# The last columns of wq's last slot, loaded as eight loads of eight partitions each onto partitions 0 to 63

## The chip, the cores and the metric

The kernel runs on one core of a Trainium2 chip. The metric is device time in microseconds (us), the median of several executions. Beside it stands one profiled execution, whose trace gives the time of each instruction and of each DMA packet. Five engines work in parallel: PE (matrix products; PEld is its weight load), DVE (vector), ACT (scalar), POOL (GpSimd) and SP (here it only issues transfers). Sixteen DMA engines move the data.

## The reference

One token `x` of 1024 numbers is normalised and goes through two branches whose results are added to `x`: attention over a cached window, and a two-layer network.

```python
xn = layernorm(x)                                   # 1024
q  = (xn @ wq).reshape(32, 128)                     # wq: 1024 x 4096
k, v = last 4096 rows of the caches                 # 4 kv heads, 8 q heads share one
o  = softmax(q @ k.T * 128**-0.5) @ v               # 32 x 128
A  = o.reshape(4096) @ wo                           # wo: 4096 x 1024
B  = gelu(layernorm(xn) @ w1 + b1) @ w2 + b2        # w1: 1024 x 3584, w2: 3584 x 1024
out = x + A + B
```

All inputs are bf16. There is one token, so every weight is used once: about 39.9 MB are read and little is computed on each byte.

## The kernel before, in words

**Data in slots.** The large arrays go through a ring of four slots of 128 partitions x 16384 bf16 (4 MB each): k, then wq in two slots, a scratch slot for the transposed k (`kt_scr`), w1 in two, v, w2 in two, wo in two. A new array takes a slot when its former content has been used. Row `8 p + c` of wq lies on partition `p`, so a partition's share of wq is eight rows, contiguous in memory: rows 0 to 3 in the first slot, rows 4 to 7 in the second (L77 to L82). One load fills one wq slot.

**Queues.** All large loads are issued by SP, in the order of the program text: k in four loads (L72), wq in two (L81), w1 in two (L202), v in three (L208), w2 in two (L216), wo in one and five pieces (L224). SP waits at an issue until its conditions hold, and everything behind it in the queue waits with it. Four small loads (x, x and b2, b1) are issued by ACT (L100 to L103). Which semaphore a load reports to is given out by the framework in program order from a set of eight, over SP's and ACT's loads together; the waits of each instruction stand in the built program.

**The work.** `x` is spread to column form `[128, 8]` by four small matmuls (L134), normalised (`layernorm`, L139 to L157) into `xn_f` and, as bf16, `xnT` (L162), and normalised again into `yT`. q is computed at L233: for each of wq's eight rows `c`, eight matmuls of 512 columns with the single column `xnT[:, c]` as weights. Their results accumulate in `accq`, whose row `32 t` and bank `b` hold columns `512 (4 b + t)` onward. ACT copies `accq` to `q_sb` (L236). w1's products (L250) accumulate in `acch` in the same manner. k is transposed on DVE in 32 x 32 blocks (L186), and sixteen copies on DVE and ACT (L195, L197) put the blocks in order in `kT`. Then come scores (L267), softmax (L270 to L292), the product with v (L306), gelu (L298), and the output product over w2 and wo (L327): its 60 chunks accumulate in `accf`, except for the last four, which go to separate accumulators (L339, L343) and are added at the end (L347, L348). Two stores write the result.

**Order.** The framework's scheduler decides the order on each engine within the limits of the dependencies; SP's loads keep the order of the text.

Of the kernel before, what the change touches and what calls it, by code (L numbers as in the profile page):

```python
# [8 lines left out]
FP32 = mybir.dt.float32  # L9
BF16 = mybir.dt.bfloat16  # L10
# [6 lines left out]
def kernel(  # L17
# [14 lines left out]
    nc = tc.nc  # L32
    P = 128
# [4 lines left out]
    NQ = A_wq.shape[1]  # L38
# [4 lines left out]
    C = D // P  # L43
    NCH = W // P
    NJQ = NQ // 512
# [8 lines left out]
    consts = ctx.enter_context(tc.tile_pool(name="consts", bufs=1))  # L54
# [4 lines left out]
    ps_f = ctx.enter_context(tc.tile_pool(name="ps_f", bufs=2, space=bass.MemoryType.PSUM))  # L59

    RING_ELEMS = 16384

    def ring_tile(name):
        return ring.tile([P, RING_ELEMS], BF16, tag="ring", name=name, align_bytes=256)

# [9 lines left out]
    wq_tiles, w1_tiles = [], []  # L75
    wq_v = A_wq.rearrange("(p c) n -> p c n", p=P)
    w1_v = B_w1.rearrange("(p c) n -> p c n", p=P)  # L77
    for i in range(2):
        t = ring_tile(f"wq{i}")
        tv = t[:].rearrange("p (r n) -> p r n", r=4)  # L80
        nc.sync.dma_start(out=tv, in_=wq_v[:, 4 * i:4 * i + 4, :])  # L81
        wq_tiles.append(tv)  # L82
    kt_scr = ring_tile("kt_scr")


    ident = consts.tile([P, P], BF16)
# [51 lines left out]
    def layernorm(src, dst, name):  # L138
        cp = small.tile([P, C], FP32, tag="ln_cp")  # L139
        sq = small.tile([P, C], FP32, tag="ln_sq")  # L140
        st = small.tile([P, 2], FP32, tag="ln_st")
        nc.scalar.activation(out=cp[:], in_=src, func=ACT.Copy, accum_out=st[:, 0:1])
        nc.scalar.activation(out=sq[:], in_=src, func=ACT.Square, accum_out=st[:, 1:2])  # L143
        tot = ps_f.tile([P, 2], FP32, tag="pf", name=name)
        nc.tensor.matmul(tot[:], lhsT=ones_f[:], rhs=st[:], start=True, stop=True)  # L145
        mv = small.tile([P, 2], FP32, tag="ln_mv")
        nc.scalar.mul(out=mv[:], in_=tot[:], mul=1.0 / n_el)
        msq = small.tile([P, 1], FP32, tag="ln_msq")
        nc.gpsimd.tensor_tensor(out=msq[:], in0=mv[:, 0:1], in1=mv[:, 0:1], op=ALU.mult)
        var = small.tile([P, 1], FP32, tag="ln_var")  # L150
        nc.gpsimd.tensor_tensor(out=var[:], in0=mv[:, 1:2], in1=msq[:], op=ALU.subtract)
        ve = small.tile([P, 1], FP32, tag="ln_ve")
        nc.gpsimd.tensor_scalar(out=ve[:], in0=var[:], scalar1=eps, scalar2=None, op0=ALU.add)
        rstd = small.tile([P, 1], FP32, tag="ln_rstd")
        nc.gpsimd.tensor_tensor(out=rstd[:], in0=ve[:], in1=mhalf[:], op=ALU.pow)
        nc.gpsimd.tensor_scalar(out=dst, in0=cp[:], scalar1=mv[:, 0:1], scalar2=rstd[:],
                                op0=ALU.subtract, op1=ALU.mult)  # L157
# [2 lines left out]
    layernorm(x_ps[:], xn_f[:], "ln_tot")  # L160
    xnT = consts.tile([P, C], BF16)
    nc.gpsimd.tensor_copy(out=xnT[:], in_=xn_f[:])  # L162
    yT = consts.tile([P, C], BF16)
    layernorm(xn_f[:], yT[:], "ln2_tot")

# [2 lines left out]
    accq = ps_acc.tile([P, 2, 512], FP32, tag="accq", name="accq")  # L168
# [5 lines left out]
    for half in range(2):  # L174
        pr = 32 * half
        for s in range(2):
            q = 2 * half + s
            nc.tensor.matmul(accf[pr:pr + 1, 256 * s:256 * s + 256], lhsT=sel8[:, q:q + 1], rhs=xb8[:],
                             start=(s == 0), stop=False, tile_position=(0, pr))
# [19 lines left out]
    for i in range(2):  # L199
        t = ring_tile(f"w1{i}")  # L200
        tv = t[:, :4 * Fd].rearrange("p (r n) -> p r n", r=4)
# [10 lines left out]
    for i in range(2):  # L212
        nr = CW2 // 2
        t = ring_tile(f"w2{i}")
        tv = t[:, :nr * D].rearrange("p (r n) -> p r n", r=nr)
# [3 lines left out]
    for i, cuts in enumerate([[0, 16], [0, 8, 12, 14, 15, 16]]):  # L219
        nr = CWO // 2  # L220
        t = ring_tile(f"wo{i}")
        tv = t[:].rearrange("p (r n) -> p r n", r=nr)
# [5 lines left out]
    for i, w3 in enumerate(wq_tiles):  # L228
        for r in range(4):
            c = 4 * i + r  # L230
            for j in range(NJQ):
                b, t = divmod(j, 4)
                nc.tensor.matmul(accq[32 * t:32 * t + 1, b, :], lhsT=xnT[:, c:c + 1], rhs=w3[:, r, j * 512:(j + 1) * 512],  # L233
                                 start=(c == 0), stop=(c == C - 1), tile_position=(0, 32 * t))
    q_sb = consts.tile([P, 2, 512], BF16)
    nc.scalar.copy(out=q_sb[:], in_=accq[:])  # L236
    qT_ps = ps_tp.tile([P, 8, P], BF16, tag="tp", name="qT_ps")
# [2 lines left out]
    for j in range(8):  # L240
        t, b = divmod(j, 2)
        nc.tensor.matmul(acch[32 * t:32 * t + 1, b, :NH], lhsT=ident[0:8, j:j + 1], rhs=b1_8[:],
                         start=True, stop=False, tile_position=(0, 32 * t))
    for i, w3 in enumerate(w1_tiles):
        for r in range(4):
            c = 4 * i + r
            for b in range(2):
                for t in range(4):
                    j = 2 * t + b
                    nc.tensor.matmul(acch[32 * t:32 * t + 1, b, :NH], lhsT=yT[:, c:c + 1], rhs=w3[:, r, j * NH:(j + 1) * NH],  # L250
                                     start=False, stop=(c == C - 1), tile_position=(0, 32 * t))
# [11 lines left out]
    for a in range(WQ4 // 512):  # L263
        for R in range(4):
            for g in range(Hkv):
                c0 = WQ4 * R + 512 * a
                nc.tensor.matmul(sp[32 * R:32 * R + 32, a, :], lhsT=qm[:, g, :], rhs=kT[:, g, c0:c0 + 512],  # L267
                                 start=(g == 0), stop=(g == Hkv - 1), tile_position=(0, 32 * R))
# [36 lines left out]
    for c in range(NCH):  # L305
        nc.tensor.matmul(o_all[:].rearrange("h g d -> h (g d)"), lhsT=eTb[:, 32 * c:32 * c + 32], rhs=v4[:, :, c, :],  # L306
                         start=(c == 0), stop=(c == NCH - 1))
# [17 lines left out]
    for idx, (kind, c, wap) in enumerate(chunk_src[:n_bulk]):  # L325
        for half in range(2):
            nc.tensor.matmul(accf[32 * half:32 * half + 1, :], lhsT=vec[kind](c), rhs=wap[:, half * 512:(half + 1) * 512],  # L327
                             start=False, stop=(idx == n_bulk - 1), tile_position=(0, 32 * half))
# [7 lines left out]
    for idx, (kind, c, wap) in enumerate(chunk_src[n_bulk:]):  # L336
        if idx == TAIL - 2:
            for half in range(2):
                nc.tensor.matmul(acct[1][32 * half:32 * half + 1, :], lhsT=ident_f[0:33, 32 * half:32 * half + 1], rhs=bulk[1][:],  # L339
                                 start=False, stop=False, tile_position=(0, 32 * half))  # L340
        for t, (n0, n1) in zip(acct, cols):
            for half in range(2):
                nc.tensor.matmul(t[32 * half:32 * half + 1, :], lhsT=vec[kind](c),  # L343
                                 rhs=wap[:, half * 512 + n0:half * 512 + n1],
                                 start=(idx == 0), stop=(idx == TAIL - 1), tile_position=(0, 32 * half))
# [36 lines left out]
```

## Time and profile before

| what | value |
|---|---|
| time, median of 3 runs | 101.81 us (101.75 to 101.86) |
| the profiled execution's own time | 102.12 us |
| its span, first to last instruction | 100.3 us |
| HBM read | 39.86 MB, 397 GB/s over the span |
| busy: PE / DVE / ACT / POOL | 45.9 / 38.2 / 30.0 / 8.2 us |
| L233, wq's 64 matmuls on PE | 7.2 us busy, 626 ns mean of one; 15.6 us idle before them, waiting for wq |
| wq's two loads, issue to landing | 24.0 us in the median |

How to read the profile: times are us from the span's start. The page cuts the span in 40 equal slices of 2.5 us and gives each a digit, the busy share in tenths. "Idle before, releaser" names what an engine waited for. A matmul's time is its own length; several run beside each other, so 32 of wq's matmuls of 626 ns each fit in 3.58 us. A load's landing is the last of its completion marks. The share of the DMA engines in a stretch can come out a little above 1, since packets overlap by a few ns.

### The profile page before, as it was taken

To read this page: it belongs to the slowest core of one execution; us is meant where nothing else is said; L and a number is where in the kernel's file an instruction comes from. 1 tells how busy PE (TensorE), PEld (TensorE's weight loads), DVE (VectorE), ACT (ScalarE), POOL (GpSimd) and SP (SyncE) were. 2 spreads that over 40 slices of the span, in tenths; PEclk is the share of its full clock that TensorE was granted. 3 is DMA by queue.
4 is the path that set the end of the run, shared out by engine and by line. 5 is a ranking of instruction groups with operands and counts; after the bars stand their busy time and mean duration, and the time that the engine had idled before them with its cause. 6 is when DMAs were issued, how large, how long until landed. Compare 5 with 4: busy or idle time off the path is not lost.

```text
span 100.3 us, 917 instructions
## 1 busy us (share of the span) xinstructions
PE 45.9 (46%) x361; PEld 17.6 (18%) x361; DVE 38.2 (38%) x26; ACT 30.0 (30%) x35; POOL 8.2 (8%) x38
## 2 busy tenths in 40 slices
PE   0005230008500940590078721999376910299990
PEld 0002200002100300230033311344132400033330
DVE  0079999999999960000001235600600000000030
ACT  5206500007999999800000029200040000000010
POOL 7901560000000000000000001000000000000000
PEclk9999999999999999999655998599999999655998
DMA  4899999999999998998999998998999999999910
GB/s 52 372 428 427 503 470 418 457 431 418 418 418 392 469 446 366 503 400 372 413 428 421 438 510 377 492 423 372 503 400 415 418 418 431 425 421 410 399 37 1
DMA packets 2951, 39.91 MB, mean 398 GB/s; under 512 B 370, under 2 KB 388, under 8 KB 772
## 3 DMA queue, kind: packets, MB, share of 16 engines
q1 hardware_dynamic: 2866, 39.85, 93.6%
q8 instruction: 3, 0.05, 0.2%
q10 hardware_dynamic: 82, 0.01, 0.1%
HBM read 39.86 MB, written 0.00 MB: 397 GB/s over the span
## 4 chain that ended last, share of the span: by engine, by line
DMA 79%; PE 17%; DVE 0%; SPq 0%; issue 0%
DMA wo<-in_A_wo_dram 33%; DMA w<-in_B_w_dram 24%; DMA wq<-in_A_wq_dram 17%; PE accf L327 9%; DMA k_sb<-in_A_k_cache_dram 5%; PE accq L233 4%; PE acch L250 3%; PE acct L343 1%; DVE res L347 0%; PE acct L339 0%; SPq L202 0%
## 5 line engine op out<-in xcount | busy, mean ns | idle before, releaser
L195 ACT COPY kT<-kt_scr 32x4096 bf16<-32x4096 bf16 x5 | 18.0, 3601 | 10.4 <-DVE kt_scr L186 10.3
L186 DVE STREAM_TRANSPOSE kt_scr<-k_sb 128x4096 bf16<-128x4096 bf16 x4 | 17.4, 4414 | 5.7 <-DMA k_sb<-in_A_k_cache_dram 5.7
L233 PE MATMUL accq<-wq,xnT 128*1 128x512 bf16 x64 | 7.2, 626 | 15.6 <-DMA wq<-in_A_wq_dram 15.6
L197 DVE COPY kT<-kt_scr 32x4096 bf16<-32x4096 bf16 x11 | 13.4, 1218 | 0.2
L327 PE MATMUL accf<-wo,o 128*1 128x512 bf16 x56 | 9.0, 498 | 6.5 <-DMA wo<-in_A_wo_dram 6.5
L250 PE MATMUL acch<-w,yT 128*1 128x448 bf16 x64 | 6.3, 572 | 10.9 <-DMA w<-in_B_w_dram 10.9
L332 DVE COPY bulk<-accf 33x320 f32<-33x320 f32 x1 | 0.5, 483 | 23.7 <-ACT bulk L331 23.7
L306 PE MATMUL o_all<-v_sb,eTb 128*32 128x512 bf16 x32 | 8.6, 435 | 1.1 <-DVE rs L290 1.1
L259 DVE COPY qm_f<-qT_ps 128x16 bf16<-128x16 bf16 x2 | 0.3, 169 | 17.9 <-PE qT_ps L254 17.9
L331 ACT COPY bulk<-accf 33x192 f32<-33x192 f32 x1 | 0.3, 313 | 22.1 <-PE accf L327 22.1
L327 PE MATMUL accf<-w,hT 128*1 128x512 bf16 x56 | 6.4, 379 | 0.9 <-DMA w<-in_B_w_dram 0.9
L233 PEld LDWEIGHTS <-xnT 128*1 128x1 bf16 x64 | 2.1, 115 | 20.6 <-issue 19.8
L276 ACT COPY m_rep<-m_row 1x128 f32<-1x128 f32 x1 | 0.3, 297 | 16.7 <-DVE m_row L274 16.7
L327 PEld LDWEIGHTS <-o 128*1 128x1 bf16 x56 | 3.0, 104 | 12.5 <-issue 10.8
L250 PEld LDWEIGHTS <-yT 128*1 128x1 bf16 x64 | 2.1, 115 | 14.7 <-issue 14.7
L306 PEld LDWEIGHTS <-eTb 128*32 128x32 bf16 x32 | 3.4, 109 | 5.8 <-issue 1.9
L297 POOL TENSOR_SCALAR zcol<-l_loc 128x1 f32<-128x1 f32 x1 | 0.2, 238 | 46.4 <-ACT e L283 46.4
L134 PE MATMUL x_ps<-x,spread 32*128 32x8 bf16 x4 | 0.2, 163 | 7.8 <-DMA x<-in_A_x_dram 7.8
L327 PEld LDWEIGHTS <-hT 128*1 128x1 bf16 x56 | 2.4, 83 | 4.4 <-issue 1.2
L313 ACT CAST o_bf<-o_f 32x128 bf16<-32x128 f32 x1 | 0.3, 297 | 9.4 <-DVE o_f L311 9.4
L309 DVE TENSOR_TENSOR o_m<-o_all,grs 32x512 f32<-32x512 f32 x1 | 0.7, 678 | 5.9 <-PE o_all L306 5.9
L145 PE MATMUL ln_tot<-st,ones_f 128*128 128x2 f32 x4 | 1.2, 363 | 2.8 <-ACT sq L143 2.8
(81 smaller groups left out, 39.9 us busy)
## 6 DMA issues: line engine op xcount, KB each, us to landing
w<-in_B_w_dram SPq DMA_DIRECT2D x4, 3584.0 KB, 19.2
wq<-in_A_wq_dram SPq DMA_DIRECT2D x2, 4096.0 KB, 24.0
k_sb<-in_A_k_cache_dram SPq DMA_DIRECT2D x4, 1024.0 KB, 9.1
wo<-in_A_wo_dram SPq DMA_DIRECT2D x1, 4096.0 KB, 33.2
v_sb<-in_A_v_cache_dram SPq DMA_DIRECT2D x1, 2048.0 KB, 19.4
v_sb<-in_A_v_cache_dram SPq DMA_DIRECT2D x2, 1024.0 KB
wo<-in_A_wo_dram SPq DMA_DIRECT2D x1, 2048.0 KB, 20.9
wo<-in_A_wo_dram SPq DMA_DIRECT2D x1, 1024.0 KB, 23.0
```

The source lines that it names most:

```text
L145: nc.tensor.matmul(tot[:], lhsT=ones_f[:], rhs=st[:], start=True, stop=True)
L186: nc.vector.transpose(out=scr[:, g, :], in_=k2[:, g, :])
L195: nc.scalar.copy(out=dst, in_=src)
L197: nc.vector.tensor_copy(out=dst, in_=src)
L233: nc.tensor.matmul(accq[32 * t:32 * t + 1, b, :], lhsT=xnT[:, c:c + 1], rhs=w3[:, r, j * 512:(j + 1) * 512], start=(c == 0), stop=(c == C ...
L250: nc.tensor.matmul(acch[32 * t:32 * t + 1, b, :NH], lhsT=yT[:, c:c + 1], rhs=w3[:, r, j * NH:(j + 1) * NH], start=False, stop=(c == C - 1) ...
L259: nc.vector.tensor_copy(out=dst, in_=src)
L306: nc.tensor.matmul(o_all[:].rearrange("h g d -> h (g d)"), lhsT=eTb[:, 32 * c:32 * c + 32], rhs=v4[:, :, c, :], start=(c == 0), stop=(c == ...
L309: nc.vector.tensor_tensor(out=o_m[:], in0=o_all[:], in1=grs[:].unsqueeze(2).to_broadcast([Hq, Hkv, Dh]), op=ALU.mult)
L327: nc.tensor.matmul(accf[32 * half:32 * half + 1, :], lhsT=vec[kind](c), rhs=wap[:, half * 512:(half + 1) * 512], start=False, stop=(idx == ...
L332: nc.vector.tensor_copy(out=bulk[0][:], in_=accf[0:33, 0:N1])
L343: nc.tensor.matmul(t[32 * half:32 * half + 1, :], lhsT=vec[kind](c), rhs=wap[:, half * 512 + n0:half * 512 + n1], start=(idx == 0), stop=( ...
```

## The change

wq's second slot is loaded without its last 1024 elements, which are columns 3072 to 4095 of row 7 of each partition. These go to a tile of their own, `wm`, with 64 partitions and two halves: half 0 of partition `p` holds the piece of partition `p`, half 1 the piece of partition `64 + p`. They come in eight loads of eight partitions, each with 2 x 2 KB per partition, issued by SP straight after wq's second slot; a load's partitions are `32 s + j`, and every fourth after it.

The products follow: row 7 has six matmuls in place of eight, and four new ones take the last two column groups from `wm`, each with 64 rows. Since half 1 now lies on partitions 0 to 63, its weights, `xnT[64:128, 7]`, have to lie there too: one matmul with the upper half of the identity moves them to PSUM, and a copy on ACT puts them in `xm`. Both wq loads are now written as one run per partition (`p (c n)`), which is the same memory.

```diff
     RING_ELEMS = 16384
+    MV = 1024
+    HP = P // 2
...
-    for i in range(2):
+    wq_run = A_wq.rearrange("(p c) n -> p (c n)", p=P)
+    for i, n_run in enumerate((RING_ELEMS, RING_ELEMS - MV)):
         t = ring_tile(f"wq{i}")
-        tv = t[:].rearrange("p (r n) -> p r n", r=4)
-        nc.sync.dma_start(out=tv, in_=wq_v[:, 4 * i:4 * i + 4, :])
-        wq_tiles.append(tv)
+        nc.sync.dma_start(out=t[:, :n_run], in_=wq_run[:, RING_ELEMS * i:RING_ELEMS * i + n_run])
+        wq_tiles.append(t[:].rearrange("p (r n) -> p r n", r=4))
+    wm = consts.tile([HP, 2, MV], BF16)
+    wm_src = wq_v[:, C - 1, NQ - MV:].rearrange("(u s e j) n -> s j e u n", u=2, s=2, j=4)
+    for s in range(2):
+        for j in range(4):
+            nc.sync.dma_start(out=wm[32 * s + j:32 * s + 32:4, :, :], in_=wm_src[s, j])
     kt_scr = ring_tile("kt_scr")
...
     nc.gpsimd.tensor_copy(out=xnT[:], in_=xn_f[:])
+    xm_ps = ps_f.tile([HP, 1], FP32, tag="pf", name="xm_ps")
+    nc.tensor.matmul(xm_ps[:], lhsT=ident[:, HP:P], rhs=xnT[:, C - 1:C], start=True, stop=True)
+    xm = consts.tile([HP, 1], BF16)
+    nc.scalar.copy(out=xm[:], in_=xm_ps[:])
...
-            for j in range(NJQ):
+            for j in range(NJQ if c < C - 1 else NJQ - MV // 512):
...
+    for u, w in enumerate((xnT[0:HP, C - 1:C], xm[:])):
+        for t in (2, 3):
+            nc.tensor.matmul(accq[32 * t:32 * t + 1, 1, :], lhsT=w, rhs=wm[:, u, 512 * (t - 2):512 * (t - 1)],
+                             start=False, stop=(u == 1), tile_position=(0, 32 * t))
     q_sb = consts.tile([P, 2, 512], BF16)
```

## The prediction

> **What bounds the kernel now.** I read the page first: the busy row of the DMA engines and the queue table.
>
> ```profile
> span 100.3 us, 917 instructions
> DMA  4899999999999998998999998998999999999910
> q1 hardware_dynamic: 2866, 39.85, 93.6%
> q8 instruction: 3, 0.05, 0.2%
> ```
>
> From slice 2 to slice 37 the sixteen DMA engines are 80 to 100% busy. One queue, SP's q1, carries 39.85 MB. The table of stages says the same for the middle of the kernel (columns: stretch and its length, busy PE, PEld, DVE, ACT, POOL, granted clock, DMA share, GB/s):
>
> ```profile
> 20.00:35.00 15.00, 6.01 (x56) 1.84 (x59) 14.85 (x11) 11.84 (x4) 0.00 (x0) 1.00 0.98 425
> 35.00:44.00 9.00, 3.87 (x44) 1.20 (x36) 1.64 (x2) 7.17 (x3) 0.00 (x0) 1.00 1.03 440
> 44.00:55.00 11.00, 4.88 (x52) 1.92 (x48) 0.26 (x2) 0.00 (x0) 0.00 (x0) 0.70 0.96 409
> 55.00:72.00 17.00, 11.41 (x69) 4.99 (x64) 5.33 (x7) 3.96 (x6) 0.53 (x2) 0.89 1.03 441
> 72.00:86.00 14.00, 6.55 (x60) 2.59 (x60) 0.85 (x1) 1.12 (x4) 0.00 (x0) 1.00 0.99 427
> ```
>
> No stage has room: whatever empties the engines at one place moves everything behind it. Then the chain that ended last, in order of time (start, length, what):
>
> ```profile
> 5.66 17.21 DMA wq<-in_A_wq_dram
> ...
> 26.97 23.73 DMA w<-in_B_w_dram
> ...
> 53.95 33.17 DMA wo<-in_A_wo_dram
> ...
> 87.16 8.98 PE accf L327 x54
> ```
>
> The chain is transfers until wo's first slot lands at 87.11. The PE tail after it runs beside the last transfers, and the last piece of wo lands at 96.85, 0.1 us before PE's last group (96.97). So the end follows the DMA stream, and stream and tail shift together.
>
> Why is the stream never empty? Because SP issues ahead, which its timeline and its waits show:
>
> ```profile
> 0.79 2.04 SPq L72 DMA_DIRECT2D k_sb<-in_A_k_cache_dram  x4
> 5.66 3.16 SPq L81 DMA_DIRECT2D wq<-in_A_wq_dram  x2
> 26.53 0.80 SPq L202 DMA_DIRECT2D w<-in_B_w_dram  x2
> ```
>
> ```profile
> SPq L81 <- DMA k_sb<-in_A_k_cache_dram: 5.3, 2, 2.8
> ```
>
> w1's two loads are issued at 26.53 and 26.97, while wq's last slot is still being read (it lands at 32.53). They cover the seam. The second fence matters most: wq's loads go to fresh ring slots, they need nothing of k, and yet the first was issued at 5.66, when k's first load had landed (5.64), and the second at 8.49, after k's second (8.47). A load's completion semaphore comes round again after eight loads, and the next load on it waits until the one before has landed.
>
> **The imbalance that the change can work on.** Each load has sixteen completion marks in the trace, one for each DMA engine. For wq's last slot they lie within 0.47 us (32.06 to 32.53). For wo's first slot thirteen lie by 85.90, one at 86.16 and two at 87.01 and 87.11: two engines run 1.1 us late. Chaining the packets (each starts some 3 ns before the end of the one ahead of it) gives sixteen strands. b1's eight 896-byte packets lie on eight of them; I call these low, the rest high. The two instruction fetches before the end (16 KB, starts 45.68 and 68.20, 0.96 us each) and all three late strands are high. So taking bytes from the high eight is aimed at the right engines. The Trainium skill (DMA: Bandwidth & Descriptors, "Why a DMA increments its semaphore by 16 and not by 1") says that an SP or ACT load of eight partitions uses the eight lowest-numbered engines. The trace agrees as far as it goes: eight 896-byte packets, one per strand.
>
> **Part by part.**
>
> - *wq's last slot shrinks* from 8 x 32 KB to 8 x 30 KB per engine. Packets of 32 KB follow each other at 1.210 us, of 28 KB at 1.059, so 2 KB less is 0.075; times 8 is **-0.60 us** on every engine. Its last mark moves from 32.53 to 31.93.
> - *Eight small loads* put 8 x 2 = 16 packets of 2 KB on each low engine. wo's 2 KB packets follow each other at 0.080, marks at 0.006: 16 x 0.080 + 8 x 0.006 = 1.33 us. Balance: high -0.60, low +0.73.
> - *SP's queue.* The eight loads stand between wq and w1, and each takes the next semaphore. In the order of the built program, the first six wait for k's last two and the four small loads (all landed by 13.2), the seventh for wq's first slot (22.87), the **eighth for wq's last slot (31.93)**. Behind it in SP's queue stand both w1 loads, then v, w2, wo. In the kernel before, w1 was issued at 26.53; now it can't be before about 32.4, when the engines have nothing left.
> - *Price of that seam.* SP reacts in 0.02 us (5.64 to 5.66): the eighth load is issued at 31.95. Issues follow each other at 0.38 to 0.47 (wo's, k's), so w1 goes at 32.33 to 32.42 (it also waits for the first small load, whose semaphore it takes; that lands by 32.2). The only load issued to idle engines is k's first: issue 0.79, first packets 1.83 to 2.19, that is 1.04 to 1.40 later, mean 1.15. w1's packets would start at about 32.38 + 1.15 = 33.53. Before, they started on the high strands at 31.73 to 31.94, mean 31.81: **+1.72**. k's first packets also took 0.87 to 1.32 us in place of 0.309, on average some 0.73 more. Whether that returns after a pause of 2 us no row shows. With all of it the seam costs +2.45; I take half, the pause being neither a first start nor a full queue: **+2.1**. Ends: the quickest issue row with the out store's 0.73 from issue to packet (98.09 to 98.82) gives 31.95 + 0.38 + 0.73 - 31.81 = +1.25; the slowest of each, 31.95 + 0.47 + 1.40 + 1.01 - 31.73 = +3.1.
> - The skill's same page ("Latency and other measured facts") gives 0.6 us to the first byte of an SP load. By it, as an estimate, w1's packets start at 33.0 and the seam costs 1.2; the trace's 1.04 at least is the measurement, and my sum goes by it.
> - *Low engines at the seam*: they end wq's part at 31.1 to 31.6, seven small loads take 1.16 more (to 32.8), the eighth starts about 33.0: done before w1's packets come. Their 0.73 us lies inside the pause. The high engines' 0.60 is lost there too: all sixteen restart together. The late strands come from the fetches at 45.7 and 68.2, behind the seam, so the 1.1 us return in full. The balance is worth **0**.
> - *PE*: two of 64 wq matmuls go, four and one for the move come: 3 x 0.112 (32 in 3.58 us) = 0.34 us. It is hidden: q is read by ACT's copy at 41.20, after ACT's long kT copies (end 41.17), and accq is ready at 36.2 now. Without that cover it would be 0.34. The small copy on ACT (a 128x32 cast took 0.186) lies in ACT's 10.3 us of waiting for the k transposes.
> - *Order on PE*: the build puts q's transposes ahead of w1's matmuls and the scores between w1's halves. w2's second and wo's first load wait for these matmuls, at some 46 and 56 us; the stream reaches those loads at 68.9 and 77.5. Cost 0, with over 20 us of cover.
>
> Sum: span 100.3 + 2.1 = 102.4, and with the 1.82 us around the span of the profiled execution (102.12 - 100.3) 104.2. That execution is 0.31 above the median of 101.81, so for the median **101.81 + 2.1 = 103.9 us**.
>
> **Rivals.**
>
> 1. *The seam stays covered, and the balance pays* (the other side). It holds if w1 is issued before wq's last packets end, about 31.6. For it: the high engines are late by 1.1 us, and 0.60 is taken from them. wo's first slot then lands at the later of 87.11 - 0.60 = 86.51 and 85.90 + 0.73 = 86.63: -0.48. The last piece goes from 96.85 to 95.74 + 0.73 = 96.47: -0.38. Time 101.4. Against: the eighth load's wait, and the L81 row, which shows that such a wait is real. Chance 0.07.
> 2. *Cold restart in full*: first packets as slow as k's, +2.5 to +3.1, time 104.3 to 104.9, middle 104.6. For it: k's row is the only restart. Against: at k everything is touched for the first time. Chance 0.13.
> 3. *The stall is taken back later*: within 0.2%. It would need idle DMA behind 34 us; the stages show shares of 0.96 to 1.03. Chance 0.03.
> 4. *PE's tail sets the end*: PE restarts at half clock (the granted clock is 0.51 from 86 to 93 us, and it changes in steps of 3.41 us). One step more at half clock would put off 3.4 / 2 = 1.7 us of PE's work, and PE's path has 0.1 us of slack at most: 103.9 + 1.6 = 105.5. Against: the idle time ahead of it (6.5 us) stays the same. Chance 0.05.
>
> **How the numbers follow.** The forecast has 0.72, with its own range 103.2 to 104.3 (seam +1.4 to +2.5). The range 103.0 to 104.9 takes in the bounds of the seam, +1.25 and +3.1, and with rival 2 holds 0.85. A difference under 0.2% (0.2 us) can't be told from none. Faster: rival 1, 0.07. Same: rival 3, 0.03. Slower: 0.72 + 0.13 + 0.05 = 0.90.
>
> **What would show it.** SP's waits should have a wait of the small loads' line for wq that ends at about 31.9, SP's timeline w1's issues at about 32.4 in place of 26.5, the busy row of the DMA engines a dent near 32 to 34 us, and PE's first w1 matmuls should start near 43.4 in place of 41.28. The small loads should show as 128 packets of 2 KB. wq's last slot should land 0.6 us earlier. If w1's issue is at 26 to 30 us, the step on SP's queue is wrong and rival 1 holds; if the dent is there and wo's first slot still lands at or before 87.1, the step on the balance is wrong.

## The result, and the profile after

The changed kernel takes 104.48 us (median of 5 runs, 104.22 to 104.81) against 101.78 (101.73 to 101.86) of the kernel before beside it: ratio 1.0266, 95% interval 1.0241 to 1.0291. It is slower. The profiled execution took 104.81, with a span of 103.0 us against 100.3. All ratios here leave out executions over 1.5% above the fastest of the same kernel, which further down are two of "ahead" and one of "behind".

From the page of the changed kernel: span, the busy row of the DMA engines, packets, and the queue of the loads.

```profile
span 103.0 us, 936 instructions
DMA  3999999999982999999899998999999999899910
DMA packets 3143, 39.91 MB, mean 387 GB/s; under 512 B 434, under 2 KB 452, under 8 KB 964
q1 hardware_dynamic: 3058, 39.85, 91.9%
```

The bytes are the same (39.85 MB). The row before had no digit below 8 between its rising and its falling end; now there is a 2 in slice 13 (30.9 to 33.5 us). The packets under 8 KB grow by 192 (772 before): 64 more are marks (under 512 B: 434 against 370), and 128 are the 2 KB packets.

SP's timeline of the changed kernel (start, length with the waits inside, line, load, how many), then SP's waits (us in total, times, longest):

```profile
5.64 2.85 SPq L83 DMA_DIRECT2D wq<-in_A_wq_dram  x2
10.64 21.88 SPq L89 DMA_DIRECT2D wm<-in_A_wq_dram  x8
32.65 0.83 SPq L213 DMA_DIRECT2D w<-in_B_w_dram  x2
```

```profile
SPq L89 <- DMA wq<-in_A_wq_dram: 15.2, 2, 8.4
SPq L89 <- DMA k_sb<-in_A_k_cache_dram: 3.0, 2, 2.1
```

The eight small loads occupy SP for 21.88 us, because two of them wait for wq, one for each slot. w1, whose first load was issued at 26.53, follows at 32.65. wq's last slot lands at 31.84, and the eighth small load is issued at 31.86. So the last load that SP could issue ahead is gone before it may send the next.

The same place in the table of stages, changed kernel (columns: stretch and its length, busy PE, PEld, DVE, ACT, POOL, granted clock, DMA share, GB/s; a packet counts where it starts, hence the 1.43):

```profile
31.00:32.00 1.00, 0.12 (x4) 0.10 (x7) 0.99 (x2) 1.00 (x1) 0.00 (x0) 0.50 0.37 135
32.00:33.00 1.00, 1.00 (x12) 0.27 (x8) 0.99 (x2) 1.00 (x1) 0.00 (x0) 0.50 0.26 94
33.00:34.00 1.00, 1.00 (x16) 0.30 (x12) 1.00 (x1) 0.99 (x2) 0.00 (x0) 0.50 1.43 377
34.00:35.00 1.00, 1.00 (x14) 0.24 (x6) 0.99 (x2) 1.00 (x1) 0.00 (x0) 0.50 0.28 115
```

For two microseconds little starts beside the small packets of the eight loads; then every engine starts one w1 packet (33.63 to 34.44, mean 33.88), these take 1.62 us on average instead of 1.06, and the second packets start at 35.49 on average. Before, those second packets started at 32.97: **2.52 us** later. The end moves by somewhat more: the chain that ended last, changed kernel (start, length, what):

```profile
8.16 23.68 DMA wq<-in_A_wq_dram
31.84 0.04 issue
31.88 3.59 PE accq L244 x30
...
36.44 26.88 DMA v_sb<-in_A_v_cache_dram
...
73.01 25.60 DMA wo<-in_A_wo_dram
...
98.65 0.60 PE acct L358 x8
...
100.22 0.48 DVE res L362
```

It still consists of transfers, 81% of the span by the page. PE's 3.59 us after wq's landing are on the list because SP's issue of v waits for `accq`; w1 is in the queue ahead of it, so the engines are not empty there. wo's first slot lands at 90.10 (87.11 before, +2.99), the last piece of wo at 99.84 (96.85, +2.99), the output store is issued at 100.77 (98.07, +2.70).

### The profile page after: what moved, and what is told of

The parts are those of the page before. It is cut to its first block, busy times and chain, and to the rows that moved or that the text cites. A ratio compares the mean times of both kernels' runs of the same rounds, so it can differ in the third digit from the quotient of the medians.

```text
span 103.0 us, 936 instructions
## 1 busy us (share of the span) xinstructions
PE 48.0 (47%) x364; PEld 18.6 (18%) x364; DVE 38.2 (37%) x26; ACT 30.1 (29%) x36; POOL 8.3 (8%) x38
## 3 DMA queue, kind: packets, MB, share of 16 engines
q1 hardware_dynamic: 3058, 39.85, 91.9%
## 4 chain that ended last, share of the span: by engine, by line
DMA 81%; PE 13%; SPq 2%; issue 1%; DVE 0%
DMA v_sb<-in_A_v_cache_dram 26%; DMA wo<-in_A_wo_dram 25%; DMA wq<-in_A_wq_dram 23%; PE o_all L321 8%; DMA k_sb<-in_A_k_cache_dram 7%; PE accq L244 3%; PE acct L358 1%; SPq L219 1%; SPq L235 1%; DVE res L362 0%; PE acct L354 0%; SPq L74 0%
## 5 line engine op out<-in xcount | busy, mean ns | idle before, releaser
L342 PE MATMUL accf<-wo,o 128*1 128x512 bf16 x56 | 8.1, 451 | 5.1 <-DMA wo<-in_A_wo_dram 5.1
L342 PE MATMUL accf<-w,hT 128*1 128x512 bf16 x56 | 8.0, 447 | 2.8 <-DMA w<-in_B_w_dram 2.8
L285 DVE TENSOR_REDUCE m_loc<-sp 128x1 f32<-128x1024 f32 x1 | 1.2, 1225 | 7.3 <-PE sp L282 7.3
L269 PE MATMUL qT_ps<-ident,q_sb 128*128 128x128 bf16 x8 | 1.0, 311 | 6.0 <-ACT q_sb L251 6.0
L265 PEld LDWEIGHTS <-yT 128*1 128x1 bf16 x64 | 2.7, 116 | 4.3 <-issue 3.5
```

The costliest lines, as they stand in the source:

```text
L269: nc.tensor.transpose(qT_ps[:, b * 4 + hh, :], q_sb[:, b, hh * Dh:(hh + 1) * Dh], ident[:])
L285: nc.vector.tensor_reduce(out=m_loc[:], in_=sp[:].rearrange("p a n -> p (a n)"), axis=AX.X, op=ALU.max)
```

## The experiments

Two theories stood against each other. **The queue's wait**: the whole cost is the eighth semaphore. It sends w1 after wq's landing, and the stream restarts cold. It would be the same whatever the eight loads carry. **The small packets themselves**: 128 packets of 2 KB and the added matmuls cost the time; then loads without bytes cost nothing, and the pieces cost it wherever they stand.

### Loads without bytes: six, seven, eight

The kernel before, with N loads added behind wq that nothing reads; each moves 8 x 2 pieces of 32 bytes.

```diff
         wq_tiles.append(tv)
+    idle = consts.tile([8, N, 2, 16], BF16)
+    for m in range(N):
+        nc.sync.dma_start(out=idle[:, m, :, :], in_=wq_v[0:8, 2 * m:2 * m + 2, 0:16] if m < 4
+                          else wq_v[8:16, 2 * m - 8:2 * m - 6, 0:16])
```

Seven:

> The kernel before, with seven loads of 8 partitions x 2 x 32 bytes (read by nothing) behind wq, so that w1's first load takes the semaphore of wq's last slot. No balance, hardly any bytes. Theory A (seam): w1's first load is issued at 32.55 instead of 26.5, its second packets start 2.8 us after that (as in the changed kernel, 32.65 to 35.47), against 32.95 in the kernel before: +2.4, less up to 0.3 that the tail takes back: 103.9 to 104.2. Theory C (bytes and 2 KB packets are the cost): 101.8 to 102.0.

Eight:

> The same with eight such loads, so that the eighth waits for wq's last slot and w1 is issued one small issue (0.79 us in the changed kernel) later still. Theory A (seam): 104.7 to 105.0, dummy7 plus 0.8; slower than the changed kernel by up to 0.6, since wq's last slot is whole here. Theory C: 101.8 to 102.1.

Six:

> The kernel before with six loads of 8 partitions x 2 x 32 bytes (read by nothing) behind wq: w1's first load then waits for wq's first slot only, its second for wq's last slot, while the first keeps the engines busy. Theory A (the wait of w1's first load is the cost): no difference from the kernel before, ratio 0.998 to 1.003. If the loads as such cost (their issues, their descriptors): each a seventh of dummy7's 1.024, so 1.020.

Measured, against the kernel before beside them: six 102.12 us, ratio 1.0007 (0.9993 to 1.0020); seven 104.49, ratio **1.0237** (1.0214 to 1.0260); eight 104.78, ratio 1.0268 (1.0248 to 1.0288). SP's timeline of the kernel with six, then seven, then eight:

```profile
10.51 3.76 SPq L85 DMA_DIRECT2D idle<-in_A_wq_dram  x6
26.15 6.63 SPq L205 DMA_DIRECT2D w<-in_B_w_dram  x2
```

```profile
10.63 12.42 SPq L85 DMA_DIRECT2D idle<-in_A_wq_dram  x7
32.51 0.84 SPq L205 DMA_DIRECT2D w<-in_B_w_dram  x2
```

```profile
10.66 22.09 SPq L85 DMA_DIRECT2D idle<-in_A_wq_dram  x8
32.86 0.83 SPq L205 DMA_DIRECT2D w<-in_B_w_dram  x2
```

And the stretch from 31 to 34 us in the table of stages, kernel before, six, seven, eight (the last two columns are the DMA share and GB/s):

```profile
31.00:34.00 3.00, 1.43 (x16) 0.51 (x19) 2.97 (x3) 2.99 (x2) 0.00 (x0) 1.00 0.89 382
```

```profile
31.00:34.00 3.00, 1.59 (x16) 0.51 (x19) 2.97 (x3) 2.99 (x2) 0.00 (x0) 0.50 0.78 307
```

```profile
31.00:34.00 3.00, 1.53 (x16) 0.51 (x19) 2.97 (x3) 3.00 (x1) 0.00 (x0) 1.00 0.55 145
```

```profile
31.00:34.00 3.00, 1.50 (x16) 0.51 (x19) 2.97 (x3) 3.00 (x1) 0.00 (x0) 0.50 0.33 78
```

Six loads cost nothing measurable. One more, of 512 bytes in all, costs 2.4 us. With six, the load whose turn meets wq's last slot is w1's second (issued near 32.4), and w1's first is out at 26.15 and covers the seam. With seven it is w1's first. With eight it is the eighth small load, and w1 comes one issue (0.35 us) later: +0.29 us. The 0.8 us expected for that last step had been taken from the change's own loads, whose issue is longer. The step from six to seven, and not a smooth rise with the number of loads, shows the wait. The second theory falls for the main cost: no 2 KB packet and no added matmul is needed for it.

### The change's loads added, wq left whole

The change's eight 2 x 2 KB loads are added to the kernel before and nothing reads them; wq keeps all its columns.

```diff
         wq_tiles.append(tv)
+    wm = consts.tile([64, 2, 1024], BF16)
+    wm_src = wq_v[:, C - 1, NQ - 1024:].rearrange("(u s e j) n -> s j e u n", u=2, s=2, j=4)
+    for s in range(2):
+        for j in range(4):
+            nc.sync.dma_start(out=wm[32 * s + j:32 * s + 32:4, :, :], in_=wm_src[s, j])
```

> The kernel before with the change's eight loads of 2 KB pieces, read by nothing, while wq is still loaded whole and computed as before: the wait and the long issue of such loads (0.79 us from the eighth to w1, against 0.39 of dummy8's), and no byte taken from the other eight engines. Theory A: w1's first load is issued at about 33.3, 0.45 us later than in dummy8: ratio dummy8's 1.027 plus 0.004, about 1.031. If taking the bytes off the other engines had been worth something in the changed kernel, extra8 would be slower than it by more than the 0.7 us by which wq's last slot lands later.

Measured: 105.12 us, ratio 1.0307 (1.0285 to 1.0329). SP's timeline of this kernel:

```profile
10.63 22.48 SPq L87 DMA_DIRECT2D wm<-in_A_wq_dram  x8
33.24 0.84 SPq L207 DMA_DIRECT2D w<-in_B_w_dram  x2
```

w1 goes 0.59 us later than in the changed kernel, since wq is 0.6 us longer, and the time is some 0.4 us longer (0.0041 x 101.8), less than the 0.7 us that would have spoken for a gain from the balance. Here the issue of the eighth small load takes 0.67 us; the eighth of 32-byte pieces took 0.27.

The three added kernels that are late and the changed one side by side, all against the kernel before (w1's second packets, mean start, 32.97 there; time from the ratio x 101.8):

| kernel | w1 issued | second packets | shift | time |
|---|---|---|---|---|
| seven, no bytes | 32.51 | 35.30 | +2.33 | +2.41 |
| eight, no bytes | 32.86 | 35.65 | +2.68 | +2.73 |
| changed kernel | 32.65 | 35.49 | +2.52 | +2.71 |
| changed loads, wq whole | 33.24 | 36.02 | +3.05 | +3.13 |

The time follows the restart within 0.2 us, and each time is known to about 0.25 us. The changed kernel is the only one of the four in which bytes of wq were moved from eight of the engines to the other eight, and it is no better for its shift than the others; the 0.4 us that the first rival had computed for the balance would have shown. The trace has the reason that the prediction gave: w1's second packets start within 0.52 us of each other (35.22 to 35.74; 32.78 to 33.23 in the kernel before), so the difference between the engines does not outlive the pause.

### The same pieces, the seam covered

Two versions of the changed kernel with the same eight loads at other places in SP's queue. "Ahead": two of them ahead of wq, six behind it. "Behind": six behind wq, the last two behind w1's first load.

```diff
+    small_loads = [(s, j) for s in range(2) for j in range(4)]
+    def load_small(pairs):
+        for s, j in pairs:
+            nc.sync.dma_start(out=wm[32 * s + j:32 * s + 32:4, :, :], in_=wm_src[s, j])
+    load_small(small_loads[:2])          # "ahead" only
     for i, n_run in enumerate((RING_ELEMS, RING_ELEMS - MV)):
...
+    load_small(small_loads[2:])          # "ahead"; [:6] in "behind"
...
         nc.sync.dma_start(out=tv, in_=w1_v[:, 4 * i:4 * i + 4, :])
+        if i == 0:                       # "behind" only
+            load_small(small_loads[6:])
```

Ahead:

> The changed kernel with the same eight small loads, the first two of them ahead of wq and six behind it; by the built order w1's first load then waits for wq's first slot, its second for wq's last slot. Theory A (the seam alone made the change slow, and the balance is worth something without it): w1's first load is issued at about 26.5 us, no dent near 32 us, wo's first slot lands near 86.6, time 101.4 us (101.2 to 101.6). Theory B (the seam made it slow, the balance is worth nothing): 101.7 to 102.0. Theory C (the small loads or their 2 KB packets on eight engines are the cost): 103.5 or more, with the stream as late as in the changed kernel.

Behind:

> The changed kernel with six small loads behind wq, and the last two behind w1's first load: that load waits for wq's first slot only, at about 26.5 us. The last two pieces then land behind w1's first slot, near 41.5 us, and q is ready some 0.5 us later, at about the time at which ACT's long copies end anyway (41.2). Theory A (seam, and the balance pays): 101.4 to 101.6. Theory B (seam, balance worth nothing): 101.7 to 102.0. Theory C (the small loads themselves): 103.5 or more.

Measured: ahead 102.39 us (101.73 to 103.55), ratio 1.0029 (1.0006 to 1.0052); behind 101.74 (101.20 to 102.73), ratio 0.9986 (0.9955 to 1.0018). SP's timeline of "ahead":

```profile
5.69 3.28 SPq L87 DMA_DIRECT2D wm<-in_A_wq_dram  x2
10.67 0.82 SPq L91 DMA_DIRECT2D wq<-in_A_wq_dram  x2
13.12 4.26 SPq L87 DMA_DIRECT2D wm<-in_A_wq_dram  x6
27.23 5.81 SPq L217 DMA_DIRECT2D w<-in_B_w_dram  x2
```

SP's timeline of "behind":

```profile
10.60 5.25 SPq L87 DMA_DIRECT2D wm<-in_A_wq_dram  x6
26.43 0.34 SPq L216 DMA_DIRECT2D w<-in_B_w_dram  x1
32.00 1.43 SPq L87 DMA_DIRECT2D wm<-in_A_wq_dram  x2
33.53 0.38 SPq L216 DMA_DIRECT2D w<-in_B_w_dram  x1
```

With w1's first load out at 26.43, nearly all of the 2.7 us is gone, though all eight loads, all 2 KB packets and all added matmuls are still there. In "ahead" the same wait has moved to another seam: the two small loads take the semaphores of k's first two loads and wq's first load that of k's third, so it goes at 10.67 instead of 5.66, just in time. Its first packets took 1.21 to 1.69 us, 1.42 on average, instead of 1.21, and wq's first slot landed at 23.55 (22.87 before), its last at 32.63 although it is shorter (32.53). That is the 0.6 us of the change lost again. The time of "ahead" lies in none of the three ranges expected for it.

Neither version gives the 101.4 us that the first rival had computed for a covered seam, as a median. So one more profile was taken of "behind", and one version was made with half as many columns moved.

"Behind", again:

> The kernel 'behind' once more, for another profile: its twelve times fall in two groups, 101.2 to 101.75 and 102.25 to 102.73, and the profile at 102.26 has its second instruction fetch on one of the eight engines that took the pieces. Theory D (the balance pays where both fetches fall on the engines that were relieved, and not where one falls on the others): in an execution near 101.4 both fetches lie on relieved strands and wo's first slot lands at 86.6 to 86.9; near 102.4 one lies on a loaded strand and it lands near 87.5. Rival: the two groups differ in PE's clock or in a wait, with the fetches in the same places.

"Behind" with 512 columns (`MV = 512`; one column group in place of two comes from `wm`):

> As 'behind' with half as many columns moved (512): relieved strands -0.30 us, loaded ones +0.37. Theory D: the groups lie closer, near 101.6 and 102.1, ratio 0.996 to 1.000. If the balance is worth nothing: 1.000 as for 'behind' (0.9986), with no less spread.

The second profile of "behind" took **101.35** us, the first 102.26. The stretch at the seam in the second, and the end of its chain:

```profile
31.00:34.00 3.00, 2.16 (x24) 0.71 (x27) 2.97 (x3) 2.99 (x2) 0.00 (x0) 1.00 1.06 448
```

```profile
70.80 24.35 DMA wo<-in_A_wo_dram
95.15 0.04 issue
95.19 0.60 PE acct L363 x8
```

In the chain of the first profile the same transfer ends 0.91 us later:

```profile
69.96 26.10 DMA wo<-in_A_wo_dram
96.06 0.04 issue
96.10 0.60 PE acct L363 x8
```

With chained packets the two are told apart by the instruction fetches, two 16 KB packets of 0.88 to 0.97 us. In the second profile both (45.08, 64.55) lie on strands without 2 KB packets, which were relieved of 0.60 us; wo's first slot lands at 86.64, its last piece at 96.38. In the first profile the second fetch (64.34) lies on a strand that carries 2 KB packets; wo's first slot lands at 87.55, its last piece at 97.30. The twelve times of "behind" lie in two groups, seven at 101.20 to 101.75 and five at 102.25 to 102.73, but only two of its executions have a profile, so that the fetches make the groups is argued and not shown. In "behind" w1's second packets start over 1.05 us (32.44 to 33.49): without the pause the difference between the engines lives on. With 512 columns the time is 101.80 (101.42 to 102.70), ratio 0.9989 (0.9964 to 1.0013), and the twelve times are spread without two clear groups, where two were expected near 101.6 and 102.1. Its one profile (101.45) fits the argument: both fetches (45.32, 64.72) lie on relieved strands, and wo's first slot lands at 86.82. Neither version can be told from the kernel before.

## Why the prediction was right

The forecast, a seam at w1 that costs 2.1 us, named the mechanism, and the runs show it; the time came out 0.58 us higher than the 103.9 forecast, within the range 103.0 to 104.9 but above the 103.2 to 104.3 that the forecast had for itself. Step by step:

- **wq's last slot**: right. Its last mark moved from 32.53 to 31.84, -0.69 us (computed -0.60).
- **SP's queue**: right. The eighth small load goes at 31.86, behind wq's landing, and the step from six to seven loads without bytes shows that this wait sets the time.
- **The issue of w1**: mis-sized. Issues were taken to follow each other at 0.38 to 0.47 us, from the rows of wo and k. The small load's issue takes 0.67, and w1 follows 0.79 behind it; with wq landing 0.09 earlier, that is 32.65 in place of 32.38, **+0.27**.
- **Issue to first packet**: 1.23 us on average against 1.15 from k's row, +0.08. The base had been taken from the high strands (31.81); over all sixteen it is 31.91, -0.10.
- **Cold first packets**: mis-sized. Half of k's +0.73 was taken; measured was 1.62 - 1.06 = +0.56, three quarters, **+0.19**. The time lies in the band that the second rival gave for the restart in full (104.3 to 104.9), though the restart alone did not bring it there.
- Sum of these: 2.1 + 0.27 + 0.08 - 0.10 + 0.19 = 2.54, and the shift of w1's second packets is 2.52. By wo's landing it is 2.99. The mean start of the sixteen engines' packets is 2.74 late at w1's fifth packets and 2.65 late in the middle of wo's first slot, so only 0.13 of the rest came on the way; the other 0.34 lies in the spread of the engines at the landing, where the last two strands are further behind the thirteenth mark than before (1.3 to 1.4 us against 1.1 to 1.2).
- **The tail**: 0.1 us of slack was given, and it gave back 0.3 (2.99 at the landing, 2.70 at the output store). Before, the last piece landed at 96.85, while PE was busy with the four small products up to its last group at 96.97; now PE is done with these before the last piece lands. The last rows of PE's timeline, kernel before, then changed kernel:

```profile
96.55 0.49 PE L339 MATMUL acct<-bulk,ident_f 33*1 33x192 f32 x4
96.97 0.60 PE L343 MATMUL acct<-wo,o 128*1 128x320 bf16 x8
```

```profile
98.65 0.60 PE L358 MATMUL acct<-wo,o 128*1 128x320 bf16 x8 [0.19 <-DMA wo<-in_A_wo_dram]
99.19 0.49 PE L354 MATMUL acct<-bulk,ident_f 33*1 33x192 f32 x4
99.60 0.66 PE L358 MATMUL acct<-wo,o 128*1 128x320 bf16 x8
```

- **The balance, worth 0**: right, by the table of the four late kernels and the start of w1's second packets. In the changed kernel two strands are again 1.3 to 1.4 us behind the thirteenth mark (88.66; the late ones 89.92 and 90.10). But the reason was narrower than it was put: that the late strands are the high ones holds for the profile before, and "behind" shows a fetch on a loaded strand. Where the balance is free to act, it gives what the first rival computed, in one execution: wo's first slot at 86.64 (computed 86.63), the last piece at 96.38 (96.47), time 101.35 (101.4). That the time agrees as well is in part luck: against the profiled execution before (102.12) it is 0.77 less, of which the last piece's landing explains 0.47.
- **PE**: the added matmuls cost nothing, right, since "behind" has them too. Its first w1 matmuls start at 45.19 and not at the 43.4 forecast, because the first instruction fetch now came at 39.07 (45.68 before), into w1's first slot:

```profile
45.19 3.16 PE L265 MATMUL acch<-w,yT 128*1 128x448 bf16 x32 [1.90 <-DMA w<-in_B_w_dram]
```

- **PE's tail at half clock** (rival four) did not happen: the granted clock from 86 to 93 us is 0.83 (0.51 before).

On the rule that a load of eight partitions uses the eight lowest-numbered engines (the Trainium skill, DMA: Bandwidth & Descriptors, "Why a DMA increments its semaphore by 16 and not by 1"), the trace agrees as to the eight: in "ahead", where the strands can be told apart, eight carry twelve 2 KB packets each between 30 and 36 us and the other eight none. Which numbers these engines have, it does not show.

The Trainium skill (DMA: Bandwidth & Descriptors, "Latency and other measured facts") gives 0.6 us to the first byte, and the prediction counted it from the start of the issue. Counted from the end of the issue to the first packet on any engine, the trace agrees: w1's first issue ends at 33.01, and its first packet starts at 33.63 (0.62 to 0.64 us in the four late kernels, 0.64 at k in the kernel before). The 1.23 us of the sum also hold 0.36 for the issue itself and 0.25 from the first engine to the mean of the sixteen.

## What to carry to other kernels

Before adding a load to a queue that issues ahead, count completion semaphores: where they come round after eight loads, a small load holds all that stands behind it until the load eight places ahead has landed, and what is behind it must not be the one that keeps the engines fed. The remedy is the order: the same eight loads cost nothing measurable once the next large load stood ahead of the one that waits. The gain from balancing the engines was lost when the stream emptied afterwards. To collect it, what makes the late engines late would also have to keep to the same engines; the two profiles of "behind" point to this, but do not prove it.

## What the runs showed of the hardware

- A stream that has run dry takes 2.8 us from the issue of the next load to its second packets, mean of the sixteen engines (2.78 to 2.84 in the four late kernels): 1.16 to 1.23 us from issue to first packet, and a first packet of 1.60 to 1.63 us in place of 1.06.
- SP's time for one issue depends on the load: 0.27 to 0.35 us for 8 x 2 pieces of 32 bytes, 0.67 to 0.84 for 8 x 2 pieces of 2 KB onto every fourth partition, 0.33 to 0.44 for a whole slot of 128 partitions (one row of 1.43 aside, w2's second load with seven). With 512 columns, that is pieces of 1 KB, it still takes 0.67 to 0.83, so halving the pieces does not make it cheaper. The step between the partitions was not varied alone, so what makes it dear stays open. The changed kernel's eight:

```profile
L89 SPq DMA_DIRECT2D wm<-in_A_wq_dram x8: 665/669/825, 10.6 to 31.9; - x8
```

- An instruction fetch of 16 KB puts its strand some 1.43 us back: 0.96 for itself, and the next packet takes 1.53 us in place of 1.06 (changed kernel, both fetches). On which strand it falls changes between executions of one kernel; what decides that was not tried.
